# A group's two filter products summed by the matmul engine instead of the vector engine, and the last two groups' forward stages put back to back

## The chip, the cores and the metric

The kernel runs on one core of one Trainium2 chip. The metric is the time of one execution on the device in microseconds (us). Most executions agree within 0.3%. Every run quoted here is marked fast in the record, so fast runs are compared with fast runs. The engines are named as in the profile: PE (matmul), PEld (its weight loads), DVE (vector), ACT (scalar), POOL (GpSimd). A copy, or eviction, moves the result of matmuls out of the memory that PE writes (PS in the code, in numbered banks) so that the bank can be written again.

## The reference, cut to what matters

Two blocks with a residual each. The first is a spectral filter (a real 2-D Fourier transform over 2048 x 576, a product with a complex filter, the inverse transform). The second is a gated feed-forward block.

```python
x = A_x                                        # (1, 2048, 576)
h = x + _A_ref(_layernorm(x), A_w_r, A_w_i)     # X = rfft2(x); X *= w_r + 1j*w_i; irfft2(X)
h2 = h + _B_ref(_layernorm(h), w_gate, w_up, w_down)   # (gelu(x@w_gate) * (x@w_up)) @ w_down
```

## The kernel before: the parts that matter

The transform along the 2048 rows is done in two factors. The change lies in the second one, the "16-point stage", which works through 16 groups of frequencies. Positions 0 to 15 are the order of work; 15 is `LAST`. Each group passes seven steps on four engines:

| step | engine | what |
|---|---|---|
| D | PE, then ACT | 6 matmuls (transform along the columns, even and odd half); ACT copies the even half |
| U | DVE | two operations: even + odd (CU), even - odd (SU) |
| B | PE, then ACT | 6 matmuls: forward 16-point transform; ACT copies it to YS |
| T | DVE | two products with the filter |
| Z | DVE | the sum of the two pairs of products: the complex result, re and im plane |
| V | PE, then ACT | 6 matmuls: inverse 16-point transform, in 3 chunks of 2; ACT copies the result |

For the last group T and Z are cut into two halves, and DVE copies the first two chunks of V, ACT the third. The next stage (I) starts when all groups' first chunks are there. In the code, `P.op(engine, ...)` issues one instruction.

```python
def st_T(i, t_, q0=0, q1=KW, hs=(0, 1)):           # products, one 128x580 instruction each
    P.op(DVE, lambda v: v.tensor_tensor(TP[:, sl, t_, :, q0:q1], YS[...], WS[...], op=ALU.mult), ...)

def st_Z(i, q0=0, q1=KW, hs=(0, 1)):               # sum
    P.op(DVE, lambda v: v.tensor_tensor(ZS[:, z3, :, q0:q1], TP[:, sl, :, 0, q0:q1], TP[:, sl, :, 1, q0:q1], op=ALU.add), ...)

def st_V(i):                                       # inverse transform: 3 chunks x 2 matmuls
    for c in range(3):
        for zp in range(2):
            P.op(PE, ... t.matmul(bank(b...), ZS[:, sl, zp, 128*c:128*c+128], VT[:, sp_, zp, :], start=(zp == 0), stop=(zp == 1)))
# ... the loop: in iteration i: D(i), U(i) [with Z(i-3) between CU and SU], B(i-2), T(i-2), V(i-4); the last iterations drain it
```

In the old drain, PE's order is D15 B13 V11 B14 V12 B15 V13 V14, three filler matmuls (nobody reads their result; they only keep PE busy), V15.

## Time and profile before

| | before |
|---|---|
| median of 3 runs | 502.81 us (502.74 to 503.13) |
| PE busy | 492.9 of 501.2 us, 98% |
| start of the last group's first D matmul | 45.85 us |
| first matmul of the next stage (I) | 53.66 us |
| the "tail": from one to the other | 7.81 us |
| from I's first matmul to the end of the span | 447.54 us |

I call the stretch between those two matmuls the tail.

From the page of the kernel before, the busy times and the chain of work that ended last:

```profile
PE 492.9 (98%) x4319; PEld 299.5 (60%) x4319; DVE 182.5 (36%) x391; ACT 158.4 (32%) x296; POOL 39.8 (8%) x49
PE 90%; DVE 7%; issue 1%; DMA 1%; SPq 0%; ACT 0%; DVEq 0%
L640 DVE TENSOR_TENSOR ZS<-TP x17: 284/449/609, 25.1 to 52.5; 128x580 bf16<-128x580 bf16 x15, 128x256 bf16<-128x256 bf16 x1, 128x324 bf16<-128x324 bf16 x1
```

(The third line is the answer for the source line of the sums: 17 of them, with minimum, median and maximum duration in ns.) An average hides the stage: DVE is busy 36% of the whole span. The busy table by stretch shows the stage itself, its tail, and the stage after it; its columns are the stretch, its length, then busy us (and instructions) of each engine, PE's granted clock and the DMA's share:

```profile
core 0: us, PE busy (x) PEld busy (x) DVE busy (x) ACT busy (x) POOL busy (x), PEclk, DMA share, GB/s
20.00:47.70 27.70, 27.53 (x252) 22.64 (x253) 26.69 (x70) 23.00 (x42) 17.18 (x19) 1.00 0.77 233
47.70:53.66 5.96, 4.75 (x42) 3.36 (x40) 5.62 (x18) 4.73 (x8) 0.91 (x2) 1.00 0.83 251
53.66:74.50 20.84, 20.84 (x173) 15.84 (x174) 13.23 (x38) 15.23 (x29) 12.70 (x14) 1.00 0.94 309
```

Up to 47.7 us PE and DVE are both full. In the tail PE has 1.21 us of holes, and after it none that the busy time shows: whatever the tail saves, the rest of the kernel should simply start earlier by that much. (A 128x289 matmul is on record for 0.29 us, but the next can start after 0.12, so a hole of less than about 0.16 us is not seen in the busy time. Experiment 6 finds one.)

The timeline of the kernel before, PE first and then DVE (start, duration, engine, line, what, and in brackets the idle time before it and who ended it):

```profile
45.85 0.91 PE L600 MATMUL PS<-FT,U 128*128 128x290 bf16 x6
48.66 0.83 PE L654 MATMUL PS<-VT,ZS 128*128 128x256 bf16 x6 [0.22 <-DVE ZS L640]
49.32 0.67 PE L626 MATMUL PS<-CUS,BT 128*128 128x289 bf16 x6
50.35 0.82 PE L654 MATMUL PS<-VT,ZS 128*128 128x256 bf16 x6 [0.35 <-DVE ZS L640]
51.63 0.83 PE L654 MATMUL PS<-VT,ZS 128*128 128x256 bf16 x6 [0.47 <-DVE ZS L640]
52.30 0.53 PE L669 MATMUL PS<-FT 128*128 128x290 bf16 x3
52.67 0.82 PE L654 MATMUL PS<-VT,ZS 128*128 128x256 bf16 x6
53.66 1.78 PE L723 MATMUL PS<-DT,V 128*128 128x289 bf16 x12 [0.17 <-DVE V L660]
...
47.78 0.45 DVE L610 TENSOR_TENSOR CUS<-ES,PS 128x290 bf16<-128x290 f32 x1
48.15 0.45 DVE L640 TENSOR_TENSOR ZS<-TP 128x580 bf16<-128x580 bf16 x1
48.52 0.44 DVE L613 TENSOR_TENSOR CUS<-ES,PS 128x288 bf16<-128x288 f32 x1
52.49 0.33 DVE L640 TENSOR_TENSOR ZS<-TP 128x324 bf16<-128x324 bf16 x1
53.09 0.76 DVE L660 CAST V<-PS 128x256 bf16<-128x256 f32 x2 [0.27 <-PE PS L654]
```

Three of PE's groups of inverse matmuls wait for a sum of DVE. DVE itself shows no idle time from 47.78 us to the last sum, which ends at 52.82. An instruction of DVE lasts 0.45 us but the next starts 0.37 us later (48.15, 48.52): they overlap, so the price of one is 0.37. The Trainium skill ("VectorE: DVE Perf Modes", section on the TRN2 errata) gives 58 cycles plus elements over the mode's factor: 58 + 580/2 cycles at the page's 0.96 GHz are 0.36 us by estimate, which agrees with the spacing, not with the duration.

### The profile page before, as it was taken

The numbers are of one execution on the slowest core, as the hardware profiler recorded it, in microseconds if no ns is written. First come the engines' busy times: TensorE is split into PE (matmuls) and PEld (weight loads), VectorE is DVE, ScalarE is ACT, GpSimd is POOL, SyncE is SP. The second block draws the span as 40 slices with busy tenths as digits, with TensorE's granted clock in tenths as the row PEclk, the third lists the DMA queues.
The fourth block names the chain that finished last, engine by engine and source line by source line (L and its number), as shares of the span: only waits on it lengthen the run. The fifth ranks groups of instructions, "written<-read, shape, count | busy, mean of one in ns | idle before, by whom it ended". The sixth has DMA issues, their size and how long they took to land.

```text
span 501.2 us, 9972 instructions
## 1 busy us (share of the span) xinstructions
PE 492.9 (98%) x4319; PEld 299.5 (60%) x4319; DVE 182.5 (36%) x391; ACT 158.4 (32%) x296; POOL 39.8 (8%) x49
## 2 busy tenths in 40 slices
PE   7999999999999999999999999999999999999998
PEld 2687674444457764444477744444677544444775
DVE  5899663344331114433311044433201233333111
ACT  7888766653220012332300023232100123233000
POOL 3645290000000000000000000000000000000000
PEclk9899999999999999999999999999999999999999
DMA  8769989001100000100000001100000000000000
GB/s 280 168 203 327 313 288 319 2 7 25 26 1 19 18 13 20 22 14 1 2 12 13 19 18 21 24 2 1 1 18 19 13 1 1 1 2 1 13 19 19
DMA packets 25948, 28.64 MB, mean 57 GB/s; under 512 B 11568, under 2 KB 19888, under 8 KB 25776
## 3 DMA queue, kind: packets, MB, share of 16 engines
q1 hardware_dynamic: 23328, 17.39, 12.1%
q0 software_dynamic: 2576, 10.62, 6.3%
q8 instruction: 34, 0.56, 0.5%
q14 instruction: 10, 0.08, 0.1%
HBM read 23.66 MB, written 2.36 MB: 52 GB/s over the span
## 4 chain that ended last, share of the span: by engine, by line
PE 90%; DVE 7%; issue 1%; DMA 1%; SPq 0%; ACT 0%; DVEq 0%
PE PS L861 56%; PE PS L884 28%; PE PS L723 3%; DVE TP L635 2%; PE PS L762 2%; DVE ST L440 1%; DMA XO<-in_A_x_dram 1%; DVE ZS L640 1%; DVE CUS L613 1%; PE PS L600 1%; DVE U L505 0%; SPq L206 0%; PE PS L807 0%; PE PS L654 0%; DVE CUS L610 0%
## 5 line engine op out<-in xcount | busy, mean ns | idle before, releaser
L861 PE MATMUL PS<-HT,WGU 64*128 64x512 bf16 x2592 | 281.9, 376 | 0.0
L861 PEld LDWEIGHTS PS<-HT,WGU 64*128 64x128 bf16 x2592 | 137.9, 94 | 142.8 <-issue 1.2
L873 ACT ACTIVATE GL<-PS 128x512 bf16<-128x512 f32 x144 | 85.9, 597 | 289.3 <-PE PS L861 288.5
L874 DVE TENSOR_TENSOR AT<-GL,PS 128x512 bf16<-128x512 bf16 x144 | 98.9, 688 | 174.2 <-PE PS L861 172.5
L884 PE MATMUL PS<-WD,AT 128*128 128x288 bf16 (+2 forms) x1152 | 141.8, 286 | 0.0
L884 PEld LDWEIGHTS PS<-WD,AT 128*128 128x128 bf16 x1152 | 111.0, 98 | 31.5 <-issue 1.7
L887 DVE TENSOR_TENSOR OS<-PS,XO 128x288 bf16<-128x288 f32 (+2 forms) x32 | 14.6, 458 | 125.8 <-PE PS L884 125.8
L674 POOL TENSOR_SCALAR WS<-WS 128x290 bf16<-128x290 bf16 x16 | 15.9, 996 | 9.6 <-DMA WS<-in_A_w_i_dram 5.9
L765 DVE SCALAR_TENSOR_TENSOR XO<-PS,XO 128x576 bf16<-128x576 f32 x16 | 12.1, 756 | 8.4 <-PE PS L762 8.4
L600 PE MATMUL PS<-FT,U 128*128 128x290 bf16 x96 | 14.4, 287 | 0.4 <-DVE U L505 0.4
L723 PE MATMUL PS<-DT,V 128*128 128x289 bf16 x96 | 14.6, 287 | 0.2 <-DVE V L660 0.2
L635 DVE TENSOR_TENSOR TP<-YS,WS 128x580 bf16<-128x580 bf16 (+2 forms) x34 | 14.1, 453 | 0.3 <-issue 0.3
L654 PE MATMUL PS<-VT,ZS 128*128 128x256 bf16 x96 | 13.1, 272 | 1.0 <-DVE ZS L640 1.0
L665 ACT ACTIVATE V<-PS 128x768 bf16<-128x768 f32 x15 | 12.2, 810 | 1.2 <-PE PS L654 1.0
L629 ACT ACTIVATE YS<-PS 128x578 bf16<-128x578 f32 x16 | 10.5, 654 | 3.3 <-PE PS L626 2.9
L732 ACT ACTIVATE GS<-PS 128x578 bf16<-128x578 f32 x15 | 9.8, 654 | 4.2 <-PE PS L723 4.1
L723 PEld LDWEIGHTS PS<-DT,V 128*128 128x128 bf16 x96 | 8.9, 97 | 3.5 <-issue 0.4
L600 PEld LDWEIGHTS PS<-FT,U 128*128 128x128 bf16 x96 | 9.2, 98 | 2.9 <-issue 0.6
L753 ACT ACTIVATE OS<-XO 128x576 bf16<-128x576 bf16 x16 | 10.8, 674 | 0.0
L626 PE MATMUL PS<-CUS,BT 128*128 128x289 bf16 (+2 forms) x96 | 10.7, 247 | 0.0
L762 PE MATMUL PS<-GS,IT 128*128 128x288 bf16 x64 | 10.5, 285 | 0.0
L483 PE MATMUL PS<-ZD 128*128 128x512 bf16 x24 | 9.1, 537 | 1.3 <-POOL ZD L377 1.3
(58 smaller groups left out, 156.6 us busy)
## 6 DMA issues: line engine op xcount, KB each, us to landing
WD<-in_B_w_down_dram POOLq DMA_DIRECT2D x9, 576.0 KB, 8.4
WGU<-in_B_w_up_dram SPq DMA_DIRECT2D x4, 1152.0 KB, 9.7
WGU<-in_B_w_gate_dram POOLq DMA_DIRECT2D x4, 1152.0 KB, 10.3
out_dram<-OS SPq DMA_DIRECT2D x30, 72.0 KB, 1.6
XO<-in_A_x_dram SPq DMA_DIRECT2D x3, 576.0 KB, 7.6
IT<-c_itab SPq DMA_DIRECT2D x1, 1024.0 KB, 7.0
HT<-HN SPq DMA_TRANSPOSE x60, 2.4
XO<-in_A_x_dram SPq DMA_DIRECT2D x2, 288.0 KB, 3.1
```

The costliest lines, as they stand in the source:

```text
L600: P.op(PE, lambda t, b=b, o=o, dt=dt, us=us, g=g: t.matmul(bank(b, 0, 128, 0, 2 * HK), U[:, us, g, :, :], FT[:, o, dt, :], start=(dt == 0) ...
L635: P.op(DVE, lambda v: v.tensor_tensor(TP[:, sl, t_, :, q0:q1], YS[:, sl, :, q0:q1], WS[:, g, w_, q0:q1], op=ALU.mult), r=[("Y", sl), ("Wn" ...
L654: P.op(PE, lambda t, b=b, o=o, c=c, zp=zp, sl=sl, sp_=sp_: t.matmul(bank(b, 0, 128, o, o + 256), ZS[:, sl, zp, 128 * c:128 * c + 128], VT[ ...
L665: P.op(ACT, lambda a, g=g, src=src: a.activation(V[:, :, :, g, :], src, ACTF.Copy), r=[("PS", bs[0]), ("PS", bs[2]), "Vfree"], w=[("V", g, ...
L674: P.op(POOL, lambda v, g=GORD[i]: v.tensor_scalar(WS[:, g, 0, :], WS[:, g, 2, :], -1.0, None, op0=ALU.mult), r=[k for k in wkeys[0 if 1 <= ...
L723: P.op(PE, lambda t, b=b, h=h, i=i, kt=kt, c=c: t.matmul(bank(b, 0, 128, 0, K2), V[:, kt, c, :, :], DT[:, 3 * h + i, 0:K2], start=(i == 0) ...
L762: P.op(PE, lambda t, b=b, h=h, i=i, c=c, rhs=rhs: t.matmul(bank(b, 0, 128, 0, 288), IT[:, h * i, c, :], rhs, start=(i == 0), stop=(i == 1) ...
L861: op = P.op(PE, lambda t, h0=h0, kt=kt, wt=wt, f=f, b=b, HT=HT, s=(half == 0 and j in (0, 5)), e=(half == 1 and j in (3, 8)): t.matmul(ban ...
L873: P.op(ACT, lambda a, s2=s2, b0=b0: a.activation(GL[:, s2, :], bank(b0), ACTF.Gelu_apprx_tanh), r=[("PS", b0)], w=[("GL", s2)])
L874: P.op(DVE, lambda v, s2=s2, b0=b0, f=f: v.tensor_tensor(AT[:, f, :], GL[:, s2, :], bank(b0 + 1), op=ALU.mult), r=[("GL", s2), ("PS", b0 + ...
L884: P.op(PE, lambda t, b=b, d0=d0, d1=d1, f=f, p=p: t.matmul(bank(b, 0, 128, 0, d1 - d0), AT[:, f, 128 * p:128 * p + 128], WD[:, f, d0:d1], ...
L887: P.op(DVE, lambda v, b=b, d0=d0, d1=d1, p=p, c=c: v.tensor_tensor(OS[:, p % 2, d0:d1], bank(b, 0, 128, 0, d1 - d0), XO[:, c, d0:d1], op=A ...
```

## The change

The intent: in the tail, take one sum (group 12's) off DVE, which has no room, and give it to PE, which has holes. A sum followed by a matmul is linear, so PE can multiply both pairs of products by the same table and let the accumulation add them: 12 matmuls instead of 6. Also the last two groups' B stages go back to back, so that the last group's copy is not stuck behind those 12, and two of the three fillers go.

```diff
-    ZS = sb.alloc("ZS", [128, 3, 2, ZW], BF16)
+    ZS = sb.alloc("ZS", [128, 4, 2, ZW], BF16)
@@ st_U
-        if i >= 3:
+        if i >= 3 and i - 3 != PESUM:          # PESUM = NG - 4 = 12
             st_Z(i - 3)
@@ st_T: group 12's products go to slots 0 and 3 of ZS instead of TP
+        out, keys = (ZS[:, 3 * t_, :, q0:q1], ...) if i == PESUM else (TP[:, sl, t_, :, q0:q1], ...)
@@ st_V
+            if i == PESUM:
+                parts = [(zp, ZS[:, 3 * zp, pl, 128*c:128*c+128], ("Z", 3 * zp, 0)) for zp in range(2) for pl in range(2)]
@@ the drain (the loop now ends at NG)
+    st_Z(NG - 3)
+    st_B(NG - 2)
+    st_T(NG - 2, 0)
+    st_T(NG - 2, 1)
+    st_B(LAST)
+    st_V(NG - 4)
+    st_V(NG - 3)
     ... T and Z of LAST and Z of NG - 2, as before ...
+    st_V(NG - 2)
+    idle_ft(1, 5)                              # was idle_ft(3, 5)
+    st_V(LAST)
```

More of the change, by code (lines that the diff above doesn't have):

```diff
@@ L616, in _build @@
     LAST = NG - 1
+    PESUM = NG - 4
+    assert PESUM % 3 == 0
     def st_B(i):
@@ L634, in st_T @@
         w_ = (slice(1, None, -1), slice(2, 0, -1))[t_]
-        P.op(DVE, lambda v: v.tensor_tensor(TP[:, sl, t_, :, q0:q1], YS[:, sl, :, q0:q1], WS[:, g, w_, q0:q1], op=ALU.mult),
-             r=[("Y", sl), ("Wn", i), "Yz", "Zz"] + wkeys[0 if 1 <= g < 9 else 1], w=[("T", sl, t_, h) for h in hs])
+        out, keys = (ZS[:, 3 * t_, :, q0:q1], [("Z", 3 * t_, h) for h in hs]) if i == PESUM else (TP[:, sl, t_, :, q0:q1], [("T", sl, t_, h) for h in hs])
+        P.op(DVE, lambda v: v.tensor_tensor(out, YS[:, sl, :, q0:q1], WS[:, g, w_, q0:q1], op=ALU.mult),
+             r=[("Y", sl), ("Wn", i), "Yz", "Zz"] + wkeys[0 if 1 <= g < 9 else 1], w=keys)
     def st_Z(i, q0=0, q1=KW, hs=(0, 1)):
@@ L652, in st_V @@
             b, o = bs[c], 256 if c == 1 and bs[0] == bs[1] else 0
-            for zp in range(2):
-                P.op(PE, lambda t, b=b, o=o, c=c, zp=zp, sl=sl, sp_=sp_: t.matmul(bank(b, 0, 128, o, o + 256), ZS[:, sl, zp, 128 * c:128 * c + 128],
-                                                                                  VT[:, sp_, zp, :], start=(zp == 0), stop=(zp == 1)),
-                     r=[("Z", sl, int(c > 0)), "Zz", "VT"], w=[("PS", b)])
+            if i == PESUM:
+                parts = [(zp, ZS[:, 3 * zp, pl, 128 * c:128 * c + 128], ("Z", 3 * zp, 0)) for zp in range(2) for pl in range(2)]
+            else:
+                parts = [(zp, ZS[:, sl, zp, 128 * c:128 * c + 128], ("Z", sl, int(c > 0))) for zp in range(2)]
+            for m, (zp, lhs, key) in enumerate(parts):
+                P.op(PE, lambda t, b=b, o=o, zp=zp, lhs=lhs, sp_=sp_, m=m, n=len(parts): t.matmul(bank(b, 0, 128, o, o + 256), lhs, VT[:, sp_, zp, :],
+                                                                                                start=(m == 0), stop=(m == n - 1)),
+                     r=[key, "Zz", "VT"], w=[("PS", b)])
             if i == LAST:
@@ L675, in _build @@
              r=[k for k in wkeys[0 if 1 <= GORD[i] < 9 else 1] if k[2] == 1] + ["Wz", ("ATS", NT - 1)], w=[("Wn", i)])
-    for i in range(NG + 4):
-        if i < NG:
-            st_D(i)
-            st_U(i)
-        if i == NG:
-            st_Z(NG - 3)
-        if 2 <= i < NG + 2:
+    for i in range(NG):
+        st_D(i)
+        st_U(i)
+        if i >= 2:
             st_B(i - 2)
-        if 2 <= i <= NG:
             st_T(i - 2, 0)
             st_T(i - 2, 1)
-        if i == NG + 1:
-            st_T(LAST, 0, 0, 128, (0,))
-            st_Z(LAST - 1)
-            st_T(LAST, 1, 0, 128, (0,))
-            st_T(LAST, 0, 128, KW, (1,))
-            st_Z(LAST, 0, 128, (0,))
-            st_T(LAST, 1, 128, KW, (1,))
-            st_Z(LAST, 128, KW, (1,))
-        if i == NG + 3:
-            idle_ft(3, 5)
         if i >= 4:
             st_V(i - 4)
+    st_Z(NG - 3)
[5 more added lines that the diff above has]
+    st_V(NG - 3)
+    st_T(LAST, 0, 0, 128, (0,))
+    st_Z(NG - 2)
+    st_T(LAST, 1, 0, 128, (0,))
+    st_T(LAST, 0, 128, KW, (1,))
+    st_Z(LAST, 0, 128, (0,))
+    st_T(LAST, 1, 128, KW, (1,))
+    st_Z(LAST, 128, KW, (1,))
+    st_V(NG - 2)
+    idle_ft(1, 5)
+    st_V(LAST)
     wdv = B_w_down[:, :].rearrange("(c p) d -> p c d", p=128)
@@ L838, in _build @@
     fdead += [("T", a, t_, h) for a in range(2) for t_ in range(2) for h in range(2)] + [("E", a) for a in range(2)]
-    fdead += [("Z", a, h) for a in range(3) for h in range(2)]
+    fdead += [("Z", a, h) for a in range(4) for h in range(2)]
     fnew = ([("AT", f) for f in range(36)] + [("GL", 0), ("GL", 1)] + [("HT", 1, i, k) for i in range(4) for k in range(5)])
```

## The prediction

> **What bounds the kernel now.** The page gives PE 98% of the 501.2 us span, and the chain of waits is 90% PE, 84% of it in the gate/up and down matmuls, which the change leaves alone. The change touches only the end of the 16-point stage. Before it, from 20 to 47.7 us, PE and DVE are both full (busy table by stretch: PE 27.53, DVE 26.69 of 27.7 us). From 47.70 to 53.66 us, where the next stage's first matmul starts, PE is busy 4.75 of 5.96 us, DVE 5.62: PE has 1.2 us of holes, and the chain runs over DVE from 24.0 to 51.6 us. So in the tail DVE is the limit, and PE has room.
>
> **What the change removes, adds, moves.**
> - DVE loses one 128x580 add (group 12's sum). In the DVE timeline it starts at 48.15 us and the next operation at 48.52: 0.37 us from start to start (0.45 is its own duration).
> - PE gets 6 more 128x256 matmuls in group 12's inverse stage. Six take 0.66 us from start to start (47.11 to 47.77), 0.11 each. The Trainium skill, "TensorE: Matmul & The Clock Gate", Back-to-back issue gap, gives 262 cycles for 256 columns, also 0.11 us: the trace agrees.
> - Two of three filler matmuls go (0.12 us each by the same timeline), so PE lengthens by about 0.4 us net, inside its holes.
> - The last group's forward matmuls move ahead of group 12's inverse ones, so its copy by ACT (50.23 us now) should come at about 49.4, and the last group's first product (50.91 us, 0.42 after its neighbour instead of 0.37) no longer waits for it: 0.05 us more.
>
> **Critical path, by estimate from these durations.** DVE: the SU subtraction at 48.15 instead of 48.52; everything after it up to the last sum moves 0.37 to 0.42 us earlier, the last sum ending near 52.40 instead of 52.82. PE: the last forward group waits for that subtraction (48.65 to 49.16), then 12 matmuls to 50.47, group 13's 6 to 51.12, group 14's when its sum is there, about 51.21. That is just level with DVE: 0.1 us of slack, and 0.2 behind it. With one filler, the last group's first pair runs at about 52.0, not 52.67, and its DVE eviction near 52.4 instead of 53.09; the second pair waits for the last sum (52.47) and is evicted at 52.9 to 53.3 instead of 53.47 to 53.9. The next stage starts near 53.0 to 53.3 instead of 53.66 to 53.9. I expect 0.5 us saved. Everything later is PE without holes (PE busy 20.84 of 20.84 us in the next stretch), and simply shifts.
>
> **Predicted time: 502.3 us**, range 501.7 to 502.9. Faster by over 2%: 0.005; within 2%: 0.985; slower by over 2%: 0.01.
>
> **What would show it.** Right: the page shows 16 sums and not 17, and 102 inverse matmuls, not 96; the add's place in the DVE timeline is empty and DVE still without holes to the last sum; the first matmul of the next stage near 53.1 us; its distance to the end of the span unchanged (447.5 us); PE waiting near 48.3 to 48.65 us. Wrong: group 14's inverse matmuls start after their sum because PE is late (12 matmuls were too many); or DVE waits for ACT's copy of the last group; or the first matmul of the next stage moves less than 0.3 us.
>
> **What would make it wrong.** The gain is 0.1%, about the spread of runs (502.74 to 503.13). The half clock that the busy table shows at 14 to 17 us can fall otherwise from run to run. PE's extra 0.35 us hole could lower the granted clock, though the Trainium skill's same page (Part 1) asks for an idle window of about 3.4 us, and this tail's holes stay under 0.5.

## The result, and the profile after

The changed kernel takes 502.41 us (median of 4 runs, 502.32 to 502.82), the kernel before 502.77 us beside it (4 runs). The ratio is 0.9994, with a 95% interval of 0.9976 to 1.0011. Ratios here are the mean time of one kernel's fast runs over that of the other's of the same rounds, so not quite the ratio of the medians. The interval holds 1. A gain of this size is visible only in the trace.

The same views of the kernel after: the sums, the stretches cut at the same points of the work, the timeline of PE, of DVE, and of ACT.

```profile
L644 DVE TENSOR_TENSOR ZS<-TP x16: 285/452/462, 25.5 to 52.4; 128x580 bf16<-128x580 bf16 x14, 128x256 bf16<-128x256 bf16 x1, 128x324 bf16<-128x324 bf16 x1
...
20.36:48.07 27.71, 27.54 (x252) 22.61 (x253) 26.70 (x70) 22.84 (x42) 16.96 (x19) 1.00 0.79 244
48.07:53.45 5.38, 5.00 (x46) 3.77 (x44) 5.25 (x17) 4.50 (x7) 0.75 (x1) 1.00 0.61 214
53.45:74.30 20.85, 20.85 (x173) 15.80 (x174) 13.27 (x38) 15.36 (x29) 12.83 (x15) 1.00 0.94 308
...
46.23 0.91 PE L600 MATMUL PS<-FT,U 128*128 128x290 bf16 x6
49.12 0.67 PE L629 MATMUL PS<-CUS,BT 128*128 128x289 bf16 x6 [0.30 <-DVE CUS L613]
49.63 2.79 PE L662 MATMUL PS<-VT,ZS 128*128 128x256 bf16 x24
52.25 0.29 PE L677 MATMUL PS<-FT 128*128 128x290 bf16 x1
53.45 1.82 PE L734 MATMUL PS<-DT,V 128*128 128x289 bf16 x12
...
48.15 0.45 DVE L610 TENSOR_TENSOR CUS<-ES,PS 128x290 bf16<-128x290 f32 x1
48.52 0.45 DVE L613 TENSOR_TENSOR CUS<-ES,PS 128x288 bf16<-128x288 f32 x1
52.44 0.33 DVE L644 TENSOR_TENSOR ZS<-TP 128x324 bf16<-128x324 bf16 x1
52.79 0.89 DVE L668 CAST V<-PS 128x256 bf16<-128x256 f32 x2
...
51.14 2.21 ACT L673 ACTIVATE V<-PS 128x768 bf16<-128x768 f32 x3 [0.60 <-PE PS L662]
```

The tail is 53.45 - 46.23 = 7.22 us, 0.59 less than before. The stretch from I's first matmul to the end is 501.0 - 53.45 = 447.55 us, as before. PE's holes in the tail fell from 1.21 us (5.96 - 4.75) to 0.38 (5.38 - 5.00). The 24 inverse matmuls of groups 12, 13 and 14 run in one piece; before, each of the three groups waited. The last sum ends 0.43 us earlier after the last group's start (52.77 - 46.23 = 6.54 us, against 52.82 - 45.85 = 6.97).

So why is the span of the profiled run only 0.2 us shorter? It entered the stage later: its first D matmul is at 20.53 us, against 20.17 before. The experiments show whether that belongs to the change.

One thing is new. ACT copies groups 12, 13 and 14 back to back (three in 2.21 us) and ends at 53.35; the next stage starts 0.10 later. DVE's first copy had ended at 53.21 (52.79 + 0.42 of one; the line gives two). ACT, not DVE, now releases the first matmul of the next stage.

### The profile page after: what moved, and what is told of

Read it like the earlier page. It is cut to its first block, busy times and chain, and to the rows that moved or that the text cites. A ratio compares the mean times of both kernels' runs of the same rounds, so it can differ in the third digit from the quotient of the medians.

```text
span 501.0 us, 9981 instructions
## 1 busy us (share of the span) xinstructions
PE 491.8 (98%) x4322; PEld 298.9 (60%) x4323; DVE 182.2 (36%) x390; ACT 158.2 (32%) x296; POOL 39.7 (8%) x49
## 4 chain that ended last, share of the span: by engine, by line
PE 90%; DVE 7%; issue 1%; DMA 1%; ACT 0%; SPq 0%; DVEq 0%
PE PS L872 56%; PE PS L895 28%; PE PS L734 3%; DVE TP L639 2%; PE PS L773 2%; DVE ST L440 1%; DVE ZS L644 1%; DMA XO<-in_A_x_dram 1%; DVE CUS L613 1%; PE PS L600 1%; DVE U L505 0%; DVE ATS L472 0%; DVE CUS L610 0%; PE PS L818 0%; DVE MV L449 0%
## 5 line engine op out<-in xcount | busy, mean ns | idle before, releaser
L494 PE MATMUL PS<-ATS,XO 128*128 128x128 bf16 (+1 forms) x80 | 7.1, 223 | 4.6 <-POOL ATS L467 2.7
```

## The experiments

Two theories to begin with. Mine: DVE bounds the tail; its missing sum is worth 0.37 us, but only if the last group's copy does not get stuck behind PE's 12 matmuls, and the fillers and the last copies give the rest. Rivals: the sum alone is the gain, or the order alone is; and for the price, that PE's 6 extra matmuls are now the limit. Kernels are compared only within the same rounds.

The results in one table. "13th matmul" is the start of the next stage's 13th matmul after the last group's first D matmul; it counts the small hole after the first matmul too. "First D" is where the stage begins. Time is the median, the ratio is to the kernel before.

| kernel | tail us | 13th matmul us | first D us | time us | ratio (95%) |
|---|---|---|---|---|---|
| before | 7.81 | 9.99 | 20.17 | 502.81 | |
| after | 7.22 | 9.44 | 20.53 | 502.41 | 0.9994 (0.9976 to 1.0011) |
| sum alone | 8.07 | 10.24 | 19.88 | 502.87 | 1.0002 (0.9990 to 1.0015) |
| order alone | 7.51 | 9.81 | 19.96 | 502.42 | 0.9995 (0.9982 to 1.0007) |
| three fillers | 7.38 | 9.55 | 19.86 | 502.22 | 0.9990 (0.9978 to 1.0003) |
| after again | 7.22 | 9.44 | 19.94 | 502.24 | 0.9990 (0.9976 to 1.0004) |
| half the sum | 7.13 | 9.44 | 20.20 | 502.39 | 0.9993 (0.9980 to 1.0007) |
| bank order | 7.22 | 9.26 | 20.06 | 501.99 | 0.9986 (0.9974 to 0.9999) |
| hole filled and bank order | 7.14 | 9.19 | 20.01 | 501.87 | 0.9984 (0.9971 to 0.9998) |
| sum on POOL | 7.59 | 9.89 | 19.91 | 502.82 | 1.0002 (0.9989 to 1.0015) |

The kernel before ran at 502.68 us (median of 9) in the first call and 502.61 in the second. The intervals of two, bank order and hole filled, leave out 1. The tail and the 13th matmul are read from one trace of each kernel.

### 1. The sum alone

The changed kernel, with the whole old drain (old order, three fillers) put back.

```diff
-    st_B(LAST)                 # before group 12's inverse stage
-    st_V(NG - 4)
+    # old drain: B(14), V(12), B(15), V(13), V(14), three fillers, V(15)
```

> Group 12's sum done by PE, but the old order of the last groups and the old three fillers. Tail = from the last group's first forward matmul to the next stage's first matmul (7.81 us before, 7.22 after). My theory: DVE's saved 0.37 us is worth nothing here, because the last group's forward matmuls now stand behind 12 inverse matmuls and not 6; ACT's copy of the last group comes about 0.1 us later than before, and DVE waits for it before the last group's first product. Tail 7.75 to 7.9, gain under 0.1 us. Rival (the sum alone is the gain): tail near 7.4, and the order brings little.

Tail 8.07 us: 0.26 worse than before, not 0.37 better. The direction was as my theory had it, the size was not: I had expected the last group's copy 0.1 us later. It starts 4.64 us after the last group's first D matmul (50.15 - 45.51), against 4.38 before (50.23 - 45.85), because its forward matmuls stand behind 12 others. The loss is there before the three fillers: group 14's inverse matmuls start 6.04 us after the last group's first D matmul (51.55 - 45.51), against 5.78 before (51.63 - 45.85). The timelines of this run, PE, ACT, then DVE:

```profile
47.94 1.47 PE L662 MATMUL PS<-VT,ZS 128*128 128x256 bf16 x12
49.25 0.67 PE L629 MATMUL PS<-CUS,BT 128*128 128x289 bf16 x6
50.15 0.65 ACT L632 ACTIVATE YS<-PS 128x578 bf16<-128x578 f32 x1
50.83 0.29 DVE L639 TENSOR_TENSOR TP<-YS,WS 128x256 bf16<-128x256 bf16 x1 [0.59 <-ACT YS L632]
51.55 0.83 PE L662 MATMUL PS<-VT,ZS 128*128 128x256 bf16 x6 [0.98 <-DVE ZS L644]
```

DVE was relieved of 0.37 us and then idle for 0.59, waiting for the last group's copy. The rival "the sum alone is the gain" falls.

### 2. The order alone

The kernel before, with the new drain and one filler; the sum stays on DVE.

> The new order and one filler, but group 12's sum still on DVE, 6 inverse matmuls for it. My theory: DVE still makes 17 sums, so the last sum ends as before less the 0.05 us wait for ACT's copy; the fillers that no longer stand before the last group give 0.1 to 0.3: tail 7.5 to 7.6. Rival (the order is the whole gain): tail 7.2 to 7.3. Other rival (the sum is the whole gain): 7.8.

Tail 7.51 us, as my theory had it. In this run the last sum ends 6.92 us after the last group's first D matmul (52.20 + 0.33 - 45.61), only 0.05 earlier than before: DVE still makes 17 sums. The order and the fillers give 0.30 of the tail, and 0.18 at the 13th matmul. Both rivals fall. The lines of this run:

```profile
51.34 0.83 PE L654 MATMUL PS<-VT,ZS 128*128 128x256 bf16 x6 [0.41 <-DVE ZS L640]
52.13 1.06 PE L654 MATMUL PS<-VT,ZS 128*128 128x256 bf16 x6
52.20 0.33 DVE L640 TENSOR_TENSOR ZS<-TP 128x324 bf16<-128x324 bf16 x1
```

The order without the fillers was not run, but these lines tell them apart. Group 14's inverse matmuls start 5.73 us after the last group's first D matmul (51.34 - 45.61), 0.05 earlier than before; the last group's, behind the fillers, start at 6.52 (52.13 - 45.61), 0.30 earlier than before (52.67 - 45.85 = 6.82). So about 0.25 of the 0.30 are the two fillers, and the order by itself, with the sum still on DVE, is worth about 0.05.

### 3. The filler matmuls

```diff
-    idle_ft(1, 5)
+    idle_ft(3, 5)
```

> The changed kernel with three fillers instead of one. My theory: PE reaches the last group's first inverse pair 0.24 us later, and its eviction by DVE ends about 0.25 later than now, 0.1 of which is hidden behind ACT's copy of group 14, which now ends last: tail 7.35 to 7.4. If fillers cost nothing: 7.22.

Tail 7.38 us: two fillers cost 0.16 us here (0.11 at the 13th matmul). Their own time is 0.24 us; at the first matmul the rest of it is hidden behind ACT's copy.

### 4. The changed kernel again

> The changed kernel again, unchanged, beside the kernel before on one chip. If the 0.6 us lies in the tail: tail 7.2 to 7.25 again, and the mean of the fast runs 0.3 to 0.7 us below before. If the part up to the first forward matmul differs from 20.17 and 20.53 us, that is the spread of the loads at the start, not the change. If the change makes the start later (the rival for the 0.36 us by which its profile begins the stage later): first forward matmul at 20.5 again.

Tail 7.22 us, and the stage begins at 19.94 us, not at 20.53. The two traces of the changed kernel agree in the tail and at the 13th matmul to 0.01 us; they are the only pair of one kernel, and so all that is known of the noise of these two marks. Over the ten traces the first D matmul lies anywhere from 19.86 to 20.53 us, in kernels that differ before it in little but the size of one early clear (and, for the sum on POOL, where two weight loads are issued). The 0.36 us by which the first profile of the change started later is this spread; the rival that the change delays the start falls. In the changed kernel's two traces the chain begins with a load of x, which landed at 4.99 us in the first and at 3.65 in the second, and six statistics instructions of DVE behind it began at 8.67 and at 8.07: the 0.59 us between the two first D matmuls are there by then. The mean of these 5 runs is 0.51 us below that of the kernel before, near what the tail says, though the interval (0.9976 to 1.0004) still holds 1.

### 5. What PE's six matmuls cost

Only one of the two pairs of products is multiplied. Its output is wrong, which doesn't matter for the time. (The comparison with the reference is too coarse to see one group's missing half.)

```diff
-                parts = [... for zp in range(2) for pl in range(2)]
+                parts = [... for zp in range(2) for pl in range(1)]
```

> The changed kernel with only one of the two products of group 12 multiplied on PE: 6 inverse matmuls for it instead of 12, wrong result on purpose. It prices PE's share of the change. My theory: PE's 0.66 us are in its own slack, but ACT copies groups 12, 13 and 14 back to back (0.70 us apart) and starts late because the 12 matmuls end late; with 6 the copy of group 14 ends about 0.1 us earlier, then DVE's copy of the last group's first chunk is the last: tail 7.13 us (7.22 now). The thirteenth matmul of the next stage stays 9.44 after the last group's first forward matmul, because the second bank's copy by DVE doesn't move. Rival (PE is the limit of the tail after the change): tail 6.6 to 6.9.

Tail 7.13 us, 13th matmul 9.44. Six matmuls, 0.66 us of PE, cost 0.09 us at the first matmul of the next stage and nothing at the 13th. They cost it through ACT, whose three copies no longer stand in one queue. Group 14's copy in this run:

```profile
50.16 1.54 ACT L673 ACTIVATE V<-PS 128x768 bf16<-128x768 f32 x2
52.13 0.81 ACT L673 ACTIVATE V<-PS 128x768 bf16<-128x768 f32 x1 [0.43 <-PE PS L662]
```

ACT waits 0.43 us for group 14 now, where it had a queue before. The rival "PE is the limit of the tail" falls: it asked for 6.6 to 6.9.

### 6. The hole after the first matmul

In the change, the next stage's second matmul starts 0.28 us after the first, not 0.12: it writes bank 1, which DVE's second copy has yet to free. So banks 2 and 3 go first.

```diff
-        for c in range(2):
-            for h in range(2):
-                i_mm(c, h, 0)
+        for c, h in ((0, 0), (1, 0), (1, 1), (0, 1)):
+            i_mm(c, h, 0)
```

> The changed kernel, and the next stage's first four matmuls in the order bank 0, 2, 3, 1 instead of 0, 1, 2, 3. In the change's profile the first starts at 7.22 and the second at 7.50, when the second chunk's copy by DVE has freed bank 1. My theory: the hole of 0.16 us goes: first matmul 7.22 still, thirteenth at 9.28 instead of 9.44. Rival (the hole is the data of the last group and not the bank): 9.44.

Tail 7.22, 13th matmul 9.26 us; the second matmul now starts 0.12 us after the first. The hole was the bank.

### 7. The hole before the last group's forward matmuls

PE waits there for DVE's subtraction. Four of group 12's twelve matmuls, whose products are ready, go into that hole; and the bank order of experiment 6.

```diff
+    st_V(NG - 4, (0,))         # first chunk
     st_B(LAST)
-    st_V(NG - 4)
+    st_V(NG - 4, (1, 2))       # the other two
```

> The order of banks of the run before, and group 12's first chunk (4 of its 12 inverse matmuls) put before the last group's forward matmuls, where PE waits 0.46 us for DVE's subtraction. My theory: group 12 ends 0.44 us earlier, ACT's three copies no longer queue, and the next stage starts at 7.13 instead of 7.22; thirteenth matmul at 9.19. Rival (no queue at ACT): 7.22 and 9.28.

Tail 7.14, 13th matmul 9.19 us. The timeline of PE in this run, whose last group's first D matmul is at 45.51 us:

```profile
47.93 0.60 PE L662 MATMUL PS<-VT,ZS 128*128 128x256 bf16 x4
48.40 0.67 PE L629 MATMUL PS<-CUS,BT 128*128 128x289 bf16 x6
48.91 1.69 PE L662 MATMUL PS<-VT,ZS 128*128 128x256 bf16 x14
50.86 0.83 PE L662 MATMUL PS<-VT,ZS 128*128 128x256 bf16 x6 [0.27 <-DVE ZS L644]
52.64 0.92 PE L735 MATMUL PS<-DT,V 128*128 128x289 bf16 x6
```

PE no longer waits before the last group's forward matmuls; it waits 0.27 us for group 14's sum instead, so the tail is DVE's again. The time is 501.87 us, the lowest of all; its interval against the kernel before (0.9971 to 0.9998) leaves out 1. Against the changed kernel, only the traces say that it is better, by 0.25 us. It was run at another time.

### 8. The sum on POOL instead

The new order, 6 matmuls for group 12, and the sum on POOL. (The first two pairs of weight loads are issued before the stage's POOL work so that they do not queue behind the sum.)

```diff
+            if i - 2 == NG - 4:
+                st_Z(i - 2, eng=POOL)
```

> Group 12's sum on POOL instead of PE, with the new order and one filler; the first two weight loads are issued ahead of it so that they don't wait. By the 1.04 us that POOL takes for a 128x512 product here, the sum takes about 1.2 us by estimate, ends about 3.3 us after the last group's first forward matmul, and is needed at 3.4. If taking the sum off DVE is what counts, wherever it goes: tail 7.1 to 7.25, as after the change. If POOL is slower, or slows DVE's own instructions (0.45 us each) while it runs: group 12's matmuls wait, tail 7.4 or more.

Tail 7.59 us: 0.08 worse than leaving the sum on DVE in the same order (7.51). POOL and DVE in this run:

```profile
47.72 1.15 POOL L640 TENSOR_TENSOR ZS<-TP 128x580 bf16<-128x580 bf16 x1 [4.85 <-DVE TP L635]
47.56 0.44 DVE L610 TENSOR_TENSOR CUS<-ES,PS 128x290 bf16<-128x290 f32 x1
47.92 0.44 DVE L613 TENSOR_TENSOR CUS<-ES,PS 128x288 bf16<-128x288 f32 x1
48.29 0.90 DVE L635 TENSOR_TENSOR TP<-YS,WS 128x580 bf16<-128x580 bf16 x1
```

POOL was in time: its sum ended at 48.87 us, and the matmuls that need it started at 49.02, as PE came free. But the product that DVE started meanwhile took 0.90 us instead of 0.45. DVE lost 0.45 us and had saved 0.37. The Trainium skill ("SBUF — State Buffer", Who interferes with whom, and the summary of rules at its end) says that a DVE instruction with two SBUF inputs and a POOL instruction that reads SBUF use one read interface, and that the second to start blocks until the first is done. The trace of this run agrees: the product, with two SBUF inputs, took twice its time and ended 0.32 us after POOL did; the two before it, with one input in PSUM, kept their 0.44 us beside POOL.

The kernel before agrees only in part. There POOL makes 128x290 products of 0.94 us in the same stage. DVE instructions with two SBUF inputs that began 0.09 to 0.14 us after one of them took 0.60 to 0.65 us, and yet ended 0.20 us before POOL's record did; and this one, which began 0.37 us after, was not held at all:

```profile
40.40 0.94 POOL L674 TENSOR_SCALAR WS<-WS 128x290 bf16<-128x290 bf16 x1
40.77 0.45 DVE L640 TENSOR_TENSOR ZS<-TP 128x580 bf16<-128x580 bf16 x1
```

So by these records DVE is not held until POOL's instruction has ended (ends on POOL are rough). That the shared read is what held the product is argued from the page and these cases; no run moved POOL's sum to another time to test it.

## Why the prediction was right

- The time: 502.3 us predicted, 502.41 measured, well within the range and far within 2%. That it came so near is partly luck: the changed kernel's own medians in two calls were 502.41 and 502.24, and by the medians the gain was 0.36 us in the first comparison, 0.44 in the second. The steps can be checked in the traces.
- DVE bounds the tail, and one sum less is worth 0.37 us plus 0.05: right. There are 16 sums and 102 inverse matmuls, as forecast, and the last sum moved 0.43 us.
- The last group's copy by ACT comes early enough in the new order: right (3.66 us after the last group's first D matmul, or 49.51 us by the clock of the kernel before; about 49.4 forecast), and experiment 1 shows that with the old drain the whole gain turns into a loss of 0.26 us. The prediction costed it as a bonus of 0.05; it is the condition.
- PE's extra matmuls fit into its holes, level with DVE: right, but with no room left. The forecast had PE 0.1 us ahead of group 14's sum; in the trace group 14's matmuls followed group 13's with no wait, 5.36 us after the last group's first D matmul, against 5.35 in experiment 5, where PE has half of group 12's work and waits for the sum. Experiment 5 prices the six at 0.09 us or nothing.
- One filler instead of three and earlier last copies give the remainder: right in sum (0.59 measured at the first matmul, about 0.5 predicted). The two fillers alone are 0.11 to 0.16 us by experiment 3, with the sum on PE.
- The next stage's first matmul "near 53.1 us": it was at 53.45, since the stage began 0.36 us later in that run. A mark that counts from the span's start was the wrong mark; counted from the last group's first D matmul the forecast (about 53.1 - 45.85 = 7.25 us) met 7.22.
- Not foreseen: ACT's queue of three copies becomes what releases the next stage, 0.09 us behind what DVE would allow.
- PE's added hole and its clock: the hole before the last forward matmuls was 0.30 us and the granted clock of the stretch stayed 1.00. The longest hole of PE in this stage in any run is 0.98 us (the sum alone), and the clock stayed 1.00 there too; an idle window of about 3.4 us, as the Trainium skill has it ("TensorE: Matmul & The Clock Gate", Part 1), was not tried. The half clock at 14 to 17 us did fall otherwise from run to run, as forecast: the mean over 10 to 20 us is 0.83 in four of the ten traces and 1.00 in six, the changed kernel's two among these.

By the 13th matmul, the parts do not add: the sum alone +0.25 us, order and fillers alone -0.18, both -0.55.

## What to carry to other kernels

Work that a linear step follows can be moved off a full vector engine into the matmul accumulation at the price of more matmuls, where PE has holes; but look at what those matmuls then stand in front of, and reorder in the same change, or the relieved engine waits for its next input. Measure a gain of a fraction of a microsecond in the trace, between two instructions of the same stage, since here the start of the stage moved by 0.59 us between two traces of one kernel. Moving the sum to POOL is not the same as removing it from DVE: here DVE lost 0.45 us beside POOL's sum and had saved 0.37.

## What the Trainium skill lacked or had wrong

- "VectorE: DVE Perf Modes", TRN2 errata: the page sets the row 58 + elements/factor against an instruction's duration and finds it too low. Here it fits the start-to-start spacing (0.37 us measured, 0.36 by the row) of overlapping instructions, whose duration is 0.45. In this tail the spacing is what one sum less was worth (the last sum moved 0.43 us, 0.05 of it by the order), not the duration.
- The same table's row for PSUM sources (120 + elements) gives 410 cycles, by estimate 0.43 us, for the 128x290 addition with one input in PSUM; its duration is 0.45 us, but its spacing to the next instruction 0.37 (47.78 to 48.15).
- "GPSIMD Engine Reference", Engine selection, has two-input operations about twice as slow as on DVE; the 128x580 sum took 1.15 us on POOL against 0.45 on DVE, 2.6 times, and 3.1 times DVE's spacing (one instruction; durations on POOL are rough).
